# Attention with normed q and k, then an MLP: first groups scaled on VectorE, first group's norm in parts, transposes placed one score later

## The chip, the cores and the metric

The kernel runs on one core of one Trainium2 chip. A core has TensorE (PE; its weight loads are shown apart as PEld), VectorE (DVE), ScalarE (ACT), GpSimd (POOL), SyncE (SP), which issues transfers, and 16 DMA engines. The metric is the device time of one execution in microseconds; the time of a kernel is the median over several executions.

## The reference

```python
q_n, k_n = rmsnorm(q, g_q), rmsnorm(k, g_k)          # x / sqrt(mean(x*x) + 1e-6) * g
scores = 1.0 / sqrt(64) * q_n @ k_n^T                # 8 batches x 12 heads, 448 x 448
attn = exp(scores - max) / (sum(exp(scores - max)) + 1e-9)
x = (attn @ v) as [8 * 448, 12 * 64]                 # 3584 x 768
h = x @ w_in                                         # 3584 x 2048
g = max(h, 0) + alpha * min(h, 0)
out = g @ w_out                                      # 3584 x 768
```

All inputs and the output are fp32; the kernel computes its matmuls in fp16 and accumulates in fp32.

## The kernel before

A *group* y is four heads of one batch: three groups (G) make a batch, 24 the whole. Its q and its k are one tile `nat` each, 128 partitions by 896 elements, fp32. For each group the kernel squares q and k (`square`, L141), sums over the head dimension (`reduce`, L151, DVE), takes the inverse root on ACT as Ln and Exp (`root`, L159), multiplies into fp16 (`scale`, L168), and transposes. Groups 0 to 5 are transposed on PE (`turn`, L188, with copies out of PSUM that also multiply k by the gain g_q * g_k); later ones by DMA transposes that SP issues (`turn_dma`, L178), after which only the gain is left for DVE (L192).

Scores of a group come in seven key tiles j: `score` (L225) makes four matmuls into one of two PSUM tiles, `soft` (L243) one exp of 128 x 896 on ACT. The sums of the exps (`den`, L269), their inverse (`log`, `invert`) and attn @ v (`attv`, L285) follow for two groups together and then for the third of a batch. Then come the MLP's units: `up` (L344) makes one of 16 feature blocks ft of h (six matmuls), a multiple by alpha on ACT (L354) into one of three `ah` buffers, and a maximum on DVE (L355) into gT; `down` (L357) makes one output tile of 128 tokens x 384 columns (16 matmuls), a copy, and two output transfers. Two PSUM banks serve `up` and `down` in turn, a further pair (`hTa`, `opa`, `hTb`) now and then.

The order is written out by hand: the program is a list of *bursts* n of two to four scores, and dictionaries say what else belongs to a burst: `prep` ahead of it, `post` behind it, `jobs` between its units, `roots`, `turns`, `dens` and `avs` by burst, `gaps` its MLP units. Each engine runs its own instructions strictly in this order, and waits where an operand or a buffer is not ready. The *lead* burst, number 10, is where the first batch's attention ends and its first feature blocks, begun before, are finished.

Transfers stand in queues too. SP issues the loads of q and k (six `nat` buffers, so that a load waits until an earlier group's tile has been scaled), the DMA transposes and the output; each waits for one of eight completion slots, used in turn. Pool issues v and the weights between its own squares and scalings: w_in in four column blocks (`load_w_in`), w_out in four quarters (`load_w_out`: two row halves of the left 384 columns, then of the right), each quarter 768 KB in SBUF. Weights and v are cast to fp16 on the way, through the queue that the profile calls software_dynamic.

While little else runs, PE gets filler matmuls (`spin`, L390). Before the change the squares of groups 0 and 1 are on ACT, the others on Pool; of the scalings q of groups 1, 2 and 3 and k of group 0 are on DVE, the others on Pool.

Of the kernel before, what the change touches and what calls it, by code (L numbers as in the profile page):

```python
# [9 lines left out]
FP32 = mybir.dt.float32  # L10
# [11 lines left out]
def kernel(  # L22
# [118 lines left out]
    def square(y, nm):  # L141
        src = nat[y, nm].rearrange("p h j d -> p (h j d)")
        sq = ld.tile([128, 2 * J, D], FP32, name="sq", tag="sq", bufs=4)
        sqf = sq.rearrange("p n d -> p (n d)")
        if y < 2:
            nc.scalar.activation(out=sqf, in_=src, func=AF.Square)  # L146
        else:
            nc.gpsimd.tensor_mul(out=sqf, in0=src, in1=src)  # L148
        sqs[y, nm] = sq
# [17 lines left out]

    def scale(y, nm):  # L168
        t = ld.tile([128, J, 2, D], FP16, name="qs", tag="qs", bufs=4)
        eng = nc.vector if (y, nm) in ((0, "k"), (1, "q"), (2, "q"), (3, "q")) else nc.gpsimd  # L170
        eng.tensor_mul(  # L171
            out=t.rearrange("p j h d -> p h j d"),
            in0=nat[y, nm],
            in1=rr_t[y][:, "qk".index(nm)].unsqueeze(3).broadcast_to((128, 2, J, D)),
        )
        qs[y, nm] = t

    def turn_dma(y):  # L178
        for nm in "qk":
# [8 lines left out]
    def turn(y):  # L188

        if y >= TD:  # L190
            t = qkT[y, "k"].rearrange("p j g c -> p (j g c)")
            nc.vector.tensor_scalar(  # L192
                out=t, in0=t, scalar1=gain[:, 0:1], scalar2=None, op0=ALU.mult
            )
            return
        if y <= G:
            ps = [psf.tile([128, 512], FP32, name="tps", tag="mm") for _ in "qk"]
        else:
            ps2 = psa.tile([128, 2, 512], FP32, name="tps2", tag="acc")
            ps = [ps2[:, 0], ps2[:, 1]]  # L200
        tps = [
            t[:, : S].bitcast(FP16).rearrange("p (j c) -> p j c", j=J) for t in ps
        ]
        for tp, nm in zip(tps, "qk"):
            for j in range(J):
                nc.tensor.transpose(  # L206
                    tp[:, j, :], qs[y, nm][:, j].rearrange("p h d -> p (h d)"), ident
                )
        for tp, nm in zip(tps, "qk"):
            t = att.tile([128, J, 2, 64], FP16, name=f"{nm}T", tag=f"{nm}T", bufs=4)  # L210
            o = t.rearrange("p j g c -> p j (g c)")
            if nm == "q" and y == 0:
                nc.scalar.copy(out=o, in_=tp)
            elif nm == "q":
                nc.vector.tensor_copy(out=o, in_=tp)
            else:
                nc.vector.tensor_scalar(
                    out=o, in0=tp, scalar1=gain[:, 0:1], scalar2=None, op0=ALU.mult
                )
            qkT[y, nm] = t  # L220
# [114 lines left out]
    def begin(ft):  # L335
# [5 lines left out]
            begun[2], begun[3] = t[:, 0], t[:, 1]  # L341
        up_part(begun[ft], 0, ft, 0, G - 1)

    def up(b, ft, spare=False):  # L344
        if b == 0 and ft in begun:
            hT = begun[ft]

            for n in {2: (2, 3), 3: ()}.get(ft, (ft,)):
                up_part(begun[n], 0, n, G - 1, G)
        else:  # L350
            hT = bank("hT", spare)
            up_part(hT, b, ft, 0, G)
        ah = ffn.tile([128, S], FP16, name="ah", tag="ah", bufs=3)
        nc.scalar.activation(out=ah, in_=hT[:, :S], func=AF.Copy, scale=alpha_sb[:, ft : ft + 1])  # L354
        nc.vector.tensor_max(out=gT[:, ft, ds((b & 1) * S, S)], in0=hT[:, :S], in1=ah)  # L355

    def down(b0, t, oh, jobs=(), spare=False):  # L357

# [82 lines left out]
                last_in[y] = n  # L441
            m += 1
    NB = len(bursts)
    prep, post, roots = {}, {}, {}

    def at(n, f, *a):
        prep.setdefault(max(int(n), 0), []).append((f, a))
# [12 lines left out]
    for y in range(G, NG):  # L460

        early = y < G + 2
        if early:
            n = turn_at[y - 1] + 1
        elif y == G + 2:
            n = den_at[G - 1]
        elif y == 2 * G:
            n = turn_at[y] - 4
        elif y % G == 1:
            n = den_at[y - 4] - 1  # L470
        elif y % G:
            n = den_at[y - G]
        else:
            n = av_at[y - 4]
        at(n - (6 if early else 4 if y <= 3 * G else 5), load_qk, y)
        for nm in "qk":
            if y != 2 * G:
                after(n - 2, square, y, nm)
            if early:
                after(n, reduce, y, nm)  # L480
            else:
                jobs.setdefault(n, []).append((reduce, (y, nm)))
        roots[n + 1] = y
    for b in range(1, B):
        at(av_at[G * b] - 6, load_v, b)

# [86 lines left out]
    load_qk(1, True)  # L573
    load_qk(2)

    spin(3)
    spin(17, False)
    ct = psf.tile([128, 512], FP32, name="ct", tag="mm")
    nc.tensor.transpose(ct[:, : NF + 2], rows, ident32[: NF + 2, : NF + 2])
    spin(1)  # L580
    for nm in "qk":
        square(0, nm)
        reduce(0, nm)
    nc.vector.tensor_copy(out=cols, in_=ct[:, : NF + 2])
    for nm in "qk":
        root(0, nm)
        scale(0, nm)
    nc.vector.tensor_mul(
        out=gain, in0=cols[:, NF : NF + 1], in1=cols[:, NF + 1 : NF + 2]
    )  # L590
    square(1, "q")
    turn(0)
    square(1, "k")
    load_v(0)
    square(2, "q")
    for nm in "qk":
        reduce(1, nm)
    after(0, root, 1)
    for nm in "qk":
        after(0, scale, 1, nm)  # L600
    after(0, square, 2, "k")
    after(0, load_w_in, 0)
    for nm in "qk":
        after(2, reduce, 2, nm)
    after(5, load_w_in, 1)
    after(7, load_w_in, 2)
    after(8, load_w_in, 3)
# [1 line left out]
        after(first + (0, 0, 2, 4)[c], load_w_out, c)  # L609
    for nm in "qk":  # L610
        after(first, square, 2 * G, nm)
    roots[3] = 2

    since = 2
    for n in range(NB):
# [4 lines left out]
        lead = n == den_at[G - 1]  # L620
        first_tiles = tiles[: 2 if lead else split.get(n, 2)]
        for t in first_tiles:
            score(*t)
            if n == den_at[G - 1] - 1 and t == tiles[-1]:
                begin(0)
                begin(1)
            elif lead and t == tiles[0]:
                soft(*t)
                den(dens[n])
                attv(avs[n], 0, True, (log, invert))  # L630
            elif lead and t == tiles[1]:
                begin(2)
        plain = lead or n not in dens and n not in avs
        wait = plain and not lead and gaps[n] and gaps[n][0][0] is up
        if lead:
            begin(3)
        for t in tiles[:1] if wait else tiles[1:2] if lead else first_tiles:
            soft(*t)
        if n in dens and not lead:
            den(dens[n])  # L640
# [15 lines left out]
        if n in roots:  # L656
# [3 lines left out]

                late = [(2, score, tiles[2]), (2, soft, tiles[2])]
            if lead or wait and y < TD:
                late += [(4 if lead else 1, f, a) for f, a in work]
            else:
                for f, a in work:
                    f(*a)
# [30 lines left out]
        for k, (f, a) in enumerate(gaps[n]):  # L697
# [3 lines left out]
            else:  # L701
                f(*a, spare)
                done += 1
                if n in jobs and not (lead and done < 4):
                    g, c = jobs[n].pop(0)
                    g(*c)
                    if not jobs[n]:
                        del jobs[n]
                while late and done == late[0][0]:
                    _, g, c = late.pop(0)  # L710
                    g(*c)
        if not gaps[n] and n in turns:
            turn(turns[n])
        for _, g, c in late:
            g(*c)
# [36 lines left out]
```

## Time and profile before

| | us |
|---|---|
| median of 7 executions | 435.91 |
| lowest, highest | 432.19, 437.68 |
| the profiled execution | 437.68 |
| its span, first to last instruction | 435.8 |
| PE busy | 417.7 (96%) |
| ACT busy | 278.8 (64%) |
| DVE busy | 203.3 (47%) |
| POOL busy | 175.1 (40%) |
| first exp starts at | 13.66 |
| first `up` matmul starts at | 35.3 |

A row of the timeline has its start, its duration, engine, line, operation, output and inputs, count, and in brackets how long the engine was idle before it and what ended that. A row of a stretch of time has the busy time of PE, PEld, DVE, ACT and POOL, the granted share of TensorE's clock, the share of the 16 DMA engines, and GB/s. Shares of DMA over 1 mean that packets overlap in an engine. Profiled times are of one execution; its own 437.68 us is what they add up to, 1.9 us of it outside the span.

### The profile page before, as it was taken

What the parts mean: (1) busy time and instruction counts of PE and PEld (TensorE: products, weight loads), DVE (VectorE), ACT (ScalarE), POOL (GpSimd) and SP (SyncE); (2) the same over time, 40 slices, a digit from 0 to 9 for tenths busy, and PEclk for the clock granted to TensorE, in tenths of its full rate; (3) what the DMA queues carried; (4) which work ended last, traced back from release to release, by engine and by line L of the source; (5) the groups of instructions that cost most, each with busy time, mean ns of one, the idle gap of its engine ahead of it and who ended that gap; (6) DMA issues with size and microseconds to landing.
All of it is one profiled execution on the core that took longest, in us unless ns stands there. A gap on an engine that the chain in (4) does not pass through costs nothing.

```text
span 435.8 us, 11487 instructions
## 1 busy us (share of the span) xinstructions
PE 417.7 (96%) x4964; PEld 216.5 (50%) x4964; DVE 203.3 (47%) x304; ACT 278.8 (64%) x385; POOL 175.1 (40%) x133
## 2 busy tenths in 40 slices
PE   7789899789999999999999999999999999999996
PEld 3344344344455545554555545554555545555564
DVE  3755763444645363455445363555444354233421
ACT  4998888548877577757757587758757587122300
POOL 4799795366084605562093605562073000000000
PEclk9999999989999999999999999999999999999999
DMA  8999999999649752789139862775054300211133
GB/s 186 232 234 218 159 212 129 233 177 213 146 69 198 150 142 33 143 174 204 25 80 199 148 149 40 134 172 129 19 96 95 80 9 21 53 41 27 29 72 74
DMA packets 70387, 53.85 MB, mean 124 GB/s; under 512 B 37424, under 2 KB 70336, under 8 KB 70336
## 3 DMA queue, kind: packets, MB, share of 16 engines
q1 hardware_dynamic: 55536, 40.19, 43.8%
q0 software_dynamic: 13984, 11.81, 18.0%
q10 hardware_dynamic: 816, 1.11, 1.1%
q8 instruction: 39, 0.64, 0.7%
q14 instruction: 12, 0.10, 0.1%
HBM read 45.62 MB, written 11.01 MB: 130 GB/s over the span
## 4 chain that ended last, share of the span: by engine, by line
PE 83%; DMA 6%; ACT 5%; DVE 4%; issue 1%; POOL 0%; SPq 0%; ACTq 0%
PE op L365 27%; PE hT L327 21%; PE hTa L327 10%; PE sc L232 7%; PE opa L365 6%; DMA w_out_sb<-in_moe_w_out_dram 5%; PE av L261 5%; PE dn L261 4%; ACT expT L246 3%; PE avb L261 2%; DMA nat<-in_k_dram 1%; DVE ss L154 1%; PE tps L206 1%; DVE gT L355 1%; DVE osb L377 1%
## 5 line engine op out<-in xcount | busy, mean ns | idle before, releaser
L246 ACT ACTIVATE expT<-sc,expb 128x896 f16<-128x896 f32 x168 | 161.5, 1003 | 40.8 <-PE sc L232 39.9
L171 POOL TENSOR_TENSOR qs<-nat,rr 128x896 f16<-128x896 f32 x44 | 76.7, 1762 | 152.2 <-issue 94.8
L365 PE MATMUL op<-w_out_sb,gT 128*128 128x384 f16 (+1 forms) x752 | 126.5, 323 | 2.8 <-DMA w_out_sb<-in_moe_w_out_dram 2.8
L365 PEld LDWEIGHTS <-gT 128*128 128x128 f16 x912 | 85.8, 98 | 68.4 <-issue 15.9
L327 PEld LDWEIGHTS <-w_in_sb 128*128 128x128 f16 x768 | 73.1, 98 | 75.3 <-issue 11.0
L327 PE MATMUL hT<-xT,w_in_sb 128*128 128x448 f16 x510 | 107.1, 353 | 2.3 <-DVE gT L355 2.2
L354 ACT ACTIVATE ah<-hT,cols 128x448 f16<-128x448 f32 x85 | 53.7, 633 | 44.9 <-PE hT L327 44.9
L355 DVE TENSOR_TENSOR gT<-hT,ah 128x448 f16<-128x448 f32 x85 | 52.8, 623 | 52.2 <-ACT ah L354 52.2
L148 POOL TENSOR_TENSOR sq<-nat 128x896 f32<-128x896 f32 x44 | 72.9, 1678 | 9.6 <-DMA nat<-in_q_dram 6.9
L377 DVE COPY osb<-op 128x384 f32<-128x384 f32 (+1 forms) x47 | 25.8, 548 | 88.8 <-PE op L365 88.8
L232 PE MATMUL sc<-qT,kT 64*32 64x448 f16 (+1 forms) x1092 | 53.6, 357 | 5.0 <-ACT expT L246 2.8
L154 DVE TENSOR_REDUCE ss<-sq 128x14 f32<-128x896 f32 x48 | 50.5, 1077 | 9.5 <-ACT sq L146 6.1
L327 PE MATMUL hTa<-xT,w_in_sb 128*128 128x448 f16 x246 | 53.2, 352 | 0.0
L354 ACT ACTIVATE ah<-hTa,cols 128x448 f16<-128x448 f32 x41 | 26.0, 634 | 31.3 <-PE hTa L327 31.3
L355 DVE TENSOR_TENSOR gT<-hTa,ah 128x448 f16<-128x448 f32 x41 | 25.5, 623 | 26.0 <-ACT ah L354 26.0
L232 PEld LDWEIGHTS <-kT 64*32 64x32 f16 (+1 forms) x1092 | 15.2, 93 | 37.1 <-issue 30.6
L365 PE MATMUL opa<-w_out_sb,gT 128*128 128x384 f16 x160 | 27.7, 326 | 0.6 <-DVE xT L312 0.6
L261 PEld LDWEIGHTS <-vt 64*32 64x32 f16 (+1 forms) x1260 | 19.4, 95 | 14.1 <-issue 3.5
L312 DVE TENSOR_TENSOR xT<-av,rden 128x896 f16<-128x896 f32 x16 | 17.5, 1092 | 18.2 <-PE av L261 14.9
L261 PE MATMUL av<-expT,vt 64*32 64x448 f16 (+1 forms) x812 | 25.4, 357 | 0.0
L261 PE MATMUL dn<-expT,ones 64*32 64x448 f16 (+1 forms) x812 | 24.2, 350 | 0.9
L278 ACT ACTIVATE rden<-dn 128x896 f32<-128x896 f32 x16 | 14.5, 907 | 7.3 <-PE dn L261 7.3
(45 smaller groups left out, 158.8 us busy)
## 6 DMA issues: line engine op xcount, KB each, us to landing
out_dram<-osb SPq DMA_DIRECT2D x109, 96.0 KB, 2.3
nat<-in_q_dram SPq DMA_DIRECT2D x46, 224.0 KB, 5.3
nat<-in_k_dram SPq DMA_DIRECT2D x46, 224.0 KB, 6.6
vt<-in_v_dram POOLq DMA_DIRECT2D x16, 336.0 KB, 7.3
w_in_sb<-in_moe_w_in_dram POOLq DMA_DIRECT2D x12, 256.0 KB, 7.3
w_out_sb<-in_moe_w_out_dram POOLq DMA_DIRECT2D x4, 768.0 KB, 13.0
nat<-in_q_dram ACTq DMA_DIRECT2D x2, 224.0 KB, 5.0
nat<-in_k_dram ACTq DMA_DIRECT2D x2, 224.0 KB, 6.5
```

Source lines behind the costliest of these rows:

```text
L148: nc.gpsimd.tensor_mul(out=sqf, in0=src, in1=src)
L154: nc.vector.tensor_reduce(out=ss_t[y][:, "qk".index(nm)].rearrange("p h j -> p (h j)").unsqueeze(2), in_=sqs[y, nm], axis=AXIS_X, op=ALU.add,)
L171: eng.tensor_mul(out=t.rearrange("p j h d -> p h j d"), in0=nat[y, nm], in1=rr_t[y][:, "qk".index(nm)].unsqueeze(3).broadcast_to((128, 2, ...
L232: nc.tensor.matmul(out=sc[ds(64 * g + m * c, m), par, :S].rearrange("p (j c) -> p j c", j=J), lhsT=kT[ds(64 * par, 64), j, g, ts(c, m)], r ...
L246: nc.scalar.activation(out=expT[y][:, j], in_=scs[y, j][:, :, :S], func=AF.Exp, scale=QK_SCALE, bias=expb[:, 0:1],)
L261: nc.tensor.matmul(out=accs[g][ds(m * h, m), :S], lhsT=weights(g, y, par, ts(c, m), j), rhs=expT[y][ds(64 * g, 64), j, par, :], start=(j = ...
L312: nc.vector.tensor_mul(out=x, in0=av[:, :, :S], in1=r)
L327: nc.tensor.matmul(out=hT[:, :S], lhsT=w_in_sb[:, g * G + i, ts(ft, 128)], rhs=xT[b][:, g, i, :], start=(i == 0 and g == 0), stop=(i == G ...
L354: nc.scalar.activation(out=ah, in_=hT[:, :S], func=AF.Copy, scale=alpha_sb[:, ft : ft + 1])
L355: nc.vector.tensor_max(out=gT[:, ft, ds((b & 1) * S, S)], in0=hT[:, :S], in1=ah)
L365: nc.tensor.matmul(out=ops[c][:, :PW], lhsT=gT[:, ft, ts(t, 128)], rhs=w_out_sb[:, ft, ds(oh * OH + c * PW, PW)], start=(ft == 0), stop=(f ...
L377: nc.vector.tensor_copy(out=o[:, ts(c, PW)], in_=ops[c][:, :PW])
```

## The change

- The squares of group 0 and of q of group 1 stay on ACT; k of group 1 is squared by Pool.
- Both q and k of groups 1 and 2 are scaled by DVE, one after the other, and so is k of group 0; q of group 0 stays on Pool, and group 3 is as before. A copy of one element on Pool (`follow`) reads the end of k's scaled tile of groups 0, 1 and 2; Pool's later work stands behind it.
- Group 0 is worked on in parts: q's square and sum in two halves, k's whole chain for key tiles 0 to 2 first and 3 to 6 after. q's transposed copy goes from ACT to DVE. k's second part is transposed behind the first burst.
- The transposes of groups 1 and 2 are made right ahead of scores (1, 0) and (1, 6).
- In the MLP's first batch the alpha multiples of blocks 2 and 3 are made by DVE, and their maxima come behind block 4's. In the lead burst the root and scalings of group 4 come after two units in place of four; the second sum and the root of group 5 come one burst later.
- q and k of group 9 are loaded behind burst den_at[3] (17), after the transposes of group 7, where they were loaded ahead of burst 16, right behind group 8. The order in which SP issues becomes: transposes of 6, load of 8, two outputs, transposes of 7, two outputs, load of 9. v of batch 1 is issued by Pool ahead of the two scalings of group 5, where it was behind them.
- The first block of w_in is issued behind burst 1 for burst 0. One of the 20 filler matmuls at the start is of the narrow kind for the wide kind, one behind the gains' transpose is gone, one stands ahead of a transpose if a burst before den_at[0] has no units.

```diff
 def square(y, nm):
-        if y < 2:
+        if (y, nm) == (1, "q"):
             nc.scalar.activation(out=sqf, in_=src, func=AF.Square)
 def scale(y, nm):
-        eng = nc.vector if (y, nm) in ((0, "k"), (1, "q"), (2, "q"), (3, "q")) else nc.gpsimd
+        eng = nc.vector if y < G or (y, nm) == (G, "q") else nc.gpsimd
...
+    def part_square(nm, h, j, eng):      # on ACT, for heads h and key tiles j
+    def part_reduce(nm, h, j):
+    def part_root(nm, j):
+    def part_scale(nm, j, n, eng):
+    def part_turn(nm, js):
+    def part_copy(nm, j, eng):
...
+    mark = cst.tile([128, 1], FP16, name="mark", tag="mark")
+    def follow(y, nm):
+        nc.gpsimd.tensor_copy(out=mark, in_=qs[y, nm][:, J - 1, 1, D - 1 : D])
 def up(b, ft, spare=False):
+        if b == 0 and ft in (2, 3):
+            nc.vector.tensor_scalar(
+                out=ah, in0=hT[:, :S], scalar1=alpha_sb[:, ft : ft + 1], scalar2=None,
+                op0=ALU.mult,
+            )
+            held.append((hT, ah, ft))
+            return
         nc.scalar.activation(out=ah, in_=hT[:, :S], func=AF.Copy, scale=alpha_sb[:, ft : ft + 1])
-        nc.vector.tensor_max(out=gT[:, ft, ds((b & 1) * S, S)], in0=hT[:, :S], in1=ah)
+        for hT, ah, ft in [(hT, ah, ft)] + (held if b == 0 and ft == 4 else []):
+            nc.vector.tensor_max(out=gT[:, ft, ds((b & 1) * S, S)], in0=hT[:, :S], in1=ah)
...
-        at(n - (6 if early else 4 if y <= 3 * G else 5), load_qk, y)
+        if y == 3 * G:
+            after(den_at[G], load_qk, y)
+        else:
+            at(n - (6 if early else 4 if y <= 3 * G else 5), load_qk, y)
...
-                jobs.setdefault(n, []).append((reduce, (y, nm)))
-        roots[n + 1] = y
+                jobs.setdefault(n + (y == G + 2 and nm == "k"), []).append((reduce, (y, nm)))
+        roots[n + 1 + (y == G + 2)] = y
...
-    for nm in "qk":
-        square(0, nm)
-        reduce(0, nm)
+    K0 = 3
+    both, full, lo, hi = slice(0, 2), slice(0, J), slice(0, K0), slice(K0, J)
+    for h in range(2):
+        part_square("q", slice(h, h + 1), full, nc.scalar)
+    for h in range(2):
+        part_reduce("q", slice(h, h + 1), full)
+    part_root("q", full)
+    part_scale("q", full, J, nc.gpsimd)
+    part_square("k", both, lo, nc.scalar)
+    part_square("k", both, hi, nc.scalar)
+    part_reduce("k", both, lo)
+    part_reduce("k", both, hi)
+    part_root("k", lo)
+    part_scale("k", lo, K0, nc.vector)
+    part_root("k", hi)
+    square(1, "q")
...
+    part_turn("q", range(J))
+    part_turn("k", range(K0))
+    part_copy("q", full, nc.vector)
+    part_copy("k", lo, nc.vector)
+    load_v(0)
+    part_scale("k", hi, J - K0, nc.vector)
+    follow(0, "k")
+    square(1, "k")
+    reduce(1, "q")
+    square(2, "q")
+    after(0, part_turn, "k", range(K0, J))
+    after(0, part_copy, "k", hi, nc.vector)
+    after(0, reduce, 1, "k")
+    mid[1] = 1
+    after(1, square, 2, "k")
+    after(1, load_w_in, 0)
     for nm in "qk":
-        after(2, reduce, 2, nm)
+        after(3, reduce, 2, nm)
...
-    roots[3] = 2
+    mid[4] = 2
...
         for t in first_tiles:
+            if t in ((1, 0), (1, J - 1)):
+                turn(1 + (t[1] > 0))
             score(*t)
...
+            if n in mid and t == tiles[-1]:
+                root(mid[n])
+                for nm in "qk":
+                    scale(mid[n], nm)
+                follow(mid[n], "k")
             soft(*t)
...
-                late += [(4 if lead else 1, f, a) for f, a in work]
+                late += [(2 if lead else 1, f, a) for f, a in work]
...
-                if n in jobs and not (lead and done < 4):
+                if n in jobs and not (lead and done < 5):
```

## The prediction

> **What bounds the kernel now.** First I read the busy rows and the chain of the page: PE is busy 417.7 of 435.8 us and the chain is 83% PE, so what can be won is about 18 us of PE idleness, 4 of them after 300 us, in the tail. Next, the engines by stretch of time, to see where that idleness lies (us; PE busy, PEld, DVE, ACT, POOL; then granted clock, DMA share, GB/s):
>
> ```profile
> PE 83%; DMA 6%; ACT 5%; DVE 4%; issue 1%; POOL 0%; SPq 0%; ACTq 0%
> ...
> 12.00:30.00 18.00, 14.21 (x165) 6.07 (x163) 11.51 (x13) 16.95 (x23) 15.53 (x13) 1.00 1.17 234
> 42.00:50.00 8.00, 6.26 (x39) 2.53 (x37) 5.21 (x9) 6.62 (x12) 4.89 (x5) 1.00 0.96 144
> 50.00:66.00 16.00, 15.24 (x123) 7.53 (x122) 10.12 (x16) 13.43 (x22) 15.99 (x14) 1.00 1.19 207
> 66.00:88.60 22.60, 18.35 (x296) 9.36 (x293) 8.88 (x12) 15.58 (x19) 10.76 (x8) 1.00 1.28 182
> 88.60:96.00 7.40, 7.37 (x63) 3.75 (x63) 3.34 (x5) 3.34 (x5) 3.82 (x5) 0.77 1.06 147
> ```
>
> From 12 to 30 us ACT is full (16.95 of 18); from 50 to 66 Pool is (15.99 of 16); from 66 to 88.6 the DMA engines are (share 1.28) and PE is idle for 4.25 us. From 96 to 300 us PE is idle for 0.6 us in all. So whatever reaches PE has to pass 88.6 us, where the chain has 21 us of transfer. The timeline there, and at two earlier places (start, duration, engine, instruction, idle before it):
>
> ```profile
> 48.80 1.30 PE L327 MATMUL hT<-xT,w_in_sb 128*128 128x448 f16 x6 [1.74 <-DVE gT L355]
> ...
> 78.30 0.38 PE L232 MATMUL sc<-qT,kT 64*64 64x448 f16 x4 [0.71 <-DVE kT L192]
> 79.30 2.76 PE L365 MATMUL opa<-w_out_sb,gT 128*128 128x384 f16 x16 [0.62 <-DVE xT L312]
> ...
> 88.63 1.50 PE L365 MATMUL op<-w_out_sb,gT 128*128 128x384 f16 x8 [2.80 <-DMA w_out_sb<-in_moe_w_out_dram]
> ...
> 90.81 2.74 PE L261 MATMUL av<-expT,vt 64*64 64x448 f16 x28
> ```
>
> PE is ready at 85.83 and waits 2.80 us for the last quarter of w_out (issued by Pool at 67.61). Then its clock drops: av takes 2.74 us where the same 28 took 1.49 at 38.78, and the eight scores beside it 0.96 for 0.57: 1.6 us more. Without stall and drop this execution is 437.68 - 2.80 - 1.6 = 433.3; the seven runs lie in two heaps, 432.19 to 433.51 and 435.91 to 437.68, as if some miss the stall. Last, the queues in 2 us windows (MB, share of 16 engines; q0 carries w_out and v, q1 q, k, output and transposes), at 68, 72 and 82 us:
>
> ```profile
> q0 software_dynamic: 368, 0.28, 89.5%
> q1 hardware_dynamic: 386, 0.10, 36.8%
> ...
> q1 hardware_dynamic: 456, 0.12, 129.5%
> q0 software_dynamic: 24, 0.02, 5.6%
> ...
> q1 hardware_dynamic: 217, 0.35, 69.9%
> q0 software_dynamic: 195, 0.15, 47.8%
> ```
>
> Alone q0 moves 0.41 MB in such a window (58 to 66 us). Beside the first packets of group 6's transposes (T6) it keeps 0.28; then, 70 to 76 us, T6 holds the engines and w_out gets 0.02; from 77 to 86 it shares with q and k of groups 8 and 9, at 0.15. That is why the last quarter (0.79 MB) takes 21 us.
>
> **What the Trainium skill says.** GPSIMD Engine Reference, Key points: Pool shares its SBUF interfaces with VectorE and contends with DVE instructions that have two SBUF inputs. The trace agrees: Pool's scaling takes 1.69 us alone (at 9.19) and 2.59 beside a DVE scaling (at 16.10), while its squares beside reductions stay at 1.68. ScalarE: Activation LUTs, What ACT_TABLE_LOAD costs: an ACTIVATE is a fixed part and 0.833 ns an element; the traced square of 896, 0.95 us, makes 448 elements 0.57 by that slope (estimate). TensorE: Matmul & The Clock Gate, What's actually happening: an idle window of about 3.4 us, free-running, halves the clock; the trace has the drop after 2.80 us and none after 1.74. DMA: Bandwidth & Descriptors, Issuing engines are not separate DMA queues: all interleave on 16 engines, as the windows show.
>
> **The change, part by part.** Durations are those of this trace; a shorter operand is scaled by its elements over a fixed 0.15 to 0.2 us.
>
> *First group in parts.* q lands at 5.42. Two half squares end at 6.0 and 6.5, their reductions (half of 1.09) at 6.65 and 7.2, root at 7.8, Pool's scaling at 9.5, against 10.88: the root no longer stands behind k's square. k lands at 7.71: squares of 3 and 4 tiles to 8.9, reductions to 9.6, scaling of 3 tiles (0.55) to 10.2, ten transposes to 10.5; cols, gain and both copies (0.17, 0.15, 0.62, 0.33) to 11.5. First score 11.55 for 13.22: 1.65 us. ACT sheds a square (0.95, to Pool) and a copy (0.91, to DVE).
>
> *Where that goes.* k's rest is scaled by 12.2; only then does the new one-element copy on Pool (named follow) let Pool square k of group 1 (1.68, to 14.05); behind it on Pool wait that square, q of group 2 and later the first w_in issue. Reduction to 15.1, root to 15.65. ACT has done three exps (0.94 each) by 14.9 and stalls 0.2. DVE now scales q and k in turn, 2 x 1.09, to 17.9 (before: both at once on two engines, to 18.7); transposes behind score (0,6) to 19.05; copies to 19.85. Exp (1,0) starts at 20.3 for 20.63: 0.3 us left. Group 2 likewise: root at 22.55, scaled by 25.3, transposes to 26.5, score, filler matmul (0.95), and exp (2,0) at 28.2 against 28.1. So by 30 us I take the lead as nil. Bounds: 0.3 us worse, if copies and squares slow each other; 1.65 better, if all of it holds.
>
> *Lead burst (42 to 52 us).* The root of group 4 comes two units earlier: ACT has it behind the exp that ends at 44.7, done at 45.3 for 47.03. Pool's queue waits on it (3.11 us idle), so its scalings, the first two w_out issues, all that follows and the q loads of SP that wait for it come 1.75 us sooner; from 47 to 68 Pool never idles, so this lasts. v of batch 1 is issued before two scalings; q0 is full then, and it costs nothing. The two copies on DVE (0.62 each) cost ACT 1.27 less, and ft 4's maximum runs ahead of the held two: done at 46.6 for 48.75, so PE's 1.74 us wait goes. Next late is ft 7, behind the scores: 1.1 us lead. Root 5, now later on ACT, takes some back where ACT is nearly full (13.43 of 16): I take 1.0 at 66 us, bounds 0.4 and 1.7.
>
> *DMA stage.* T6 lands at 76.0 for 77.8, so the 0.71 wait goes and the 0.62 stays (xT waits for it): PE reaches the last quarter at 85.83 - 1.6 = 84.2. The quarter is issued at 65.9, and T6 is through at about 74.5. Then q and k of group 8 (0.92 MB) and w_out share as at 82 us: group 8 is done at 80, w_out has 0.43 MB and lacks 0.33. Group 9's load, moved behind the transposes of group 7 (T7), is out of the way. But T7, in the trace issued at 83.10 behind group 9's loads, which wait for free completion slots, now issues at 73 to 76 and follows group 8 in the ring. If T7 starts as T6 did (q0 kept 0.28 MB in 2 us), 0.33 MB take 2.3 us: 82.3, before PE is there. If T7 holds the engines as T6 did at 70 to 76, w_out waits. I take the first; both ends are kept.
>
> *Sum.* No stall (2.80), no drop (1.6), arrival 1.6 earlier: 437.68 - 6.0 = 431.7 us. Against the median of 435.91, which holds the stall, 4.2 us or 1.0% less.
>
> **Rivals.** *T7 takes group 9's place.* For: 70 to 76 us, where T6 left q0 0.02 MB. T7 from 80 to 86.5, then 0.33 MB at the shared 0.16 in 2 us less what trickled: about 88. PE stands 3.8 us and the clock drops: 437.68 - 0.6 = 437.1, or some 436.4 with the trickle; no change. Against: T7 alone took 3.2 us later in the run (124 to 127). *The front's gain holds.* For: ACT is the bound there. Against: the scaling chain above. 431.7 - 1.65 = 430.0. *Slower: T7 smothers w_out.* T6's packets beside w_out spanned 66 to 77.8, 11.8 us. From 80 that is 91.8, plus 0.33 MB at 0.2 MB a us: 93.4, 4.8 us later than now: 442.5. It decides from a landing at 91.3. For: same ring, same place. Against: T6 met two quarters, T7 half of one. *The roots are not earlier* (ACT late at 44.7): Pool keeps its times, which ends in one of the first two cases.
>
> **How the numbers follow.** Forecast 0.50 (430.8 to 433.5), T7 in group 9's place 0.28 (435.3 to 437.8), front holds 0.12 (430.0), smothered 0.10. A measurement of this kernel tells about 1% from no change: faster means below 431.55, slower above 440.3. Slightly under half of the forecast's case lies below 431.55 (0.23), with the front 0.35; smothered 0.10; the rest 0.55. The range, 430.0 to 437.5, leaves out the last case and the edge of the second.
>
> **What would show it.** Right: first exp near 12.0 but exp (2,0) still near 28; no wait at ft 6; w_out's first issue near 48.6; the second half of op at 84 to 85 without a DMA wait and with full clock behind it. Wrong: a DMA wait over 2 us at that op with T7's small packets beside it; or q0 and T7 sharing the engines evenly, but exp (2,0) later than 29, which would mean that DVE's two scalings in turn cost more than Pool's hold frees.

## The result, and the profile after

| | before | after |
|---|---|---|
| median, us (executions) | 433.22 (64) | 434.50 (27) |
| lowest, highest | 431.14, 439.04 | 431.02, 437.33 |
| ratio of after to before | | 1.0021, 95% interval 1.0006 to 1.0036 |
| the profiled execution, its span | 437.68, 435.8 | 434.08, 432.1 |

The change makes no difference of 1%; the interval leaves a small loss, 0.1 to 0.4%. The 64 executions of the kernel before include the seven shown ahead of the prediction, whose median of 435.91 was high. So was their profiled execution, a slow one, 1.5% above the fastest of the 64: a second profile of the unchanged kernel (below, "the kernel before once more") has a span of 431.0 us. Medians of the kernel before differ by a few tenths of a microsecond from one group of runs to the next, so I compare by ratios. A ratio is not the quotient of the two medians: here the two differ by as much as 0.0025 (the lead edits below have a ratio of 0.9999, by medians 1.0015), so differences smaller than that say little.

The same views of the changed kernel: first the shares of the chain that ended last.

```profile
PE 80%; DMA 6%; DVE 4%; ACT 4%; POOL 3%; issue 1%; SPq 1%; ACTq 1%; POOLq 0%
```

Then its engines by stretch of time (us; busy PE, PEld, DVE, ACT, POOL; granted clock, DMA share, GB/s).

```profile
12.00:30.00 18.00, 13.61 (x178) 6.02 (x185) 13.12 (x15) 15.95 (x23) 12.41 (x14) 1.00 1.14 244
42.00:50.00 8.00, 7.83 (x64) 3.80 (x63) 7.08 (x12) 6.87 (x11) 7.06 (x8) 1.00 1.07 177
50.00:66.00 16.00, 15.18 (x109) 7.36 (x108) 10.96 (x17) 14.10 (x22) 15.97 (x12) 1.00 1.23 202
66.00:88.60 22.60, 20.54 (x334) 10.31 (x332) 8.61 (x13) 15.88 (x19) 6.69 (x4) 1.00 1.29 183
88.60:96.00 7.40, 5.89 (x39) 2.85 (x38) 3.32 (x5) 3.35 (x8) 5.92 (x5) 1.00 1.03 221
```

The lead burst is fuller (42 to 50 us: PE busy 7.83 for 6.26). In the transfer stage, 66 to 88.6 us, PE is busy for 20.54 us, more than the 18.35 of the first profile of before, which holds the stall, but less than the 22.28 of the second, which has none. And from 88.6 to 96 us PE now stands for 1.5 us, and in neither profile of before does it stand there. PE's timeline of the changed kernel at these places (start, duration, instruction, and in brackets the idle time before it with what ended it):

```profile
49.03 1.30 PE L393 MATMUL hT<-xT,w_in_sb 128*128 128x448 f16 x6
...
76.11 0.38 PE L298 MATMUL sc<-qT,kT 64*64 64x448 f16 x4
77.11 2.76 PE L442 MATMUL opa<-w_out_sb,gT 128*128 128x384 f16 x16 [0.62 <-DVE xT L378]
...
84.46 1.46 PE L442 MATMUL op<-w_out_sb,gT 128*128 128x384 f16 x8 [0.82 <-DMA w_out_sb<-in_moe_w_out_dram]
...
95.03 2.62 PE L393 MATMUL hT<-xT,w_in_sb 128*128 128x448 f16 x12 [1.51 <-DVE osb L454]
...
98.31 1.29 PE L393 MATMUL hT<-xT,w_in_sb 128*128 128x448 f16 x6 [0.16 <-DVE gT L432]
```

The 1.74 us wait of the lead burst is gone, the one on the last quarter of w_out is 0.82 for 2.80 with full clock behind it, and at 95.03 there is a new wait of 1.51 us, for the copy `osb`. VectorE's and then Pool's timeline of the changed kernel show what held that copy:

```profile
91.79 1.09 DVE L154 TENSOR_REDUCE ss<-sq 128x14 f32<-128x896 f32 x1 [2.83 <-POOL sq L148]
93.43 1.09 DVE L154 TENSOR_REDUCE ss<-sq 128x14 f32<-128x896 f32 x1 [0.55 <-POOL sq L148]
94.43 0.55 DVE L454 COPY osb<-op 128x384 f32<-128x384 f32 x1
```

```profile
90.08 3.32 POOL L148 TENSOR_TENSOR sq<-nat 128x896 f32<-128x896 f32 x2 [6.72 <-DMA nat<-in_q_dram]
```

Group 9's q arrives only at 90 us. Its squares wait for it on Pool, its sums wait for the squares on VectorE, and the copy that frees a bank for PE stands behind the sums.

Last, the queues of the changed kernel in 2 us windows at 66, 68, 72 and 82 us (packets, MB, share of the 16 engines):

```profile
q0 software_dynamic: 369, 0.28, 89.3%
q1 hardware_dynamic: 403, 0.10, 37.5%
...
q1 hardware_dynamic: 655, 0.16, 85.3%
q0 software_dynamic: 206, 0.15, 48.1%
...
q1 hardware_dynamic: 141, 0.05, 61.8%
q0 software_dynamic: 137, 0.11, 57.7%
...
q1 hardware_dynamic: 390, 0.10, 85.6%
q0 software_dynamic: 65, 0.05, 17.7%
```

Group 6's transposes (T6) no longer push w_out to nothing at 72 us, but neither queue moves much there: 0.16 MB in 2 us for the two together, against 0.38 at 66 us.

### The profile page after: what moved, and what is told of

It is laid out like the page before. It is cut to its first block, busy times and chain, and to the rows that moved or that the text cites. A ratio compares the mean times of both kernels' runs of the same rounds, so it can differ in the third digit from the quotient of the medians.

```text
span 432.1 us, 11497 instructions
## 1 busy us (share of the span) xinstructions
PE 415.7 (96%) x4961; PEld 216.1 (50%) x4961; DVE 206.9 (48%) x313; ACT 276.7 (64%) x385; POOL 172.0 (40%) x135
## 4 chain that ended last, share of the span: by engine, by line
PE 80%; DMA 6%; DVE 4%; ACT 4%; POOL 3%; issue 1%; SPq 1%; ACTq 1%; POOLq 0%
PE op L442 26%; PE hT L393 20%; PE hTa L393 10%; PE sc L298 6%; PE opa L442 6%; PE dn L327 4%; PE av L327 4%; DMA kT<-qs 3%; PE avb L327 2%; POOL sq L148 2%; DMA nat<-in_q_dram 2%; DVE ss L154 1%; ACT expT L312 1%; DMA nat<-in_k_dram 1%; DVE osb L454 1%
## 5 line engine op out<-in xcount | busy, mean ns | idle before, releaser
L171 POOL TENSOR_TENSOR qs<-nat,rr 128x896 f16<-128x896 f32 x41 | 69.7, 1721 | 138.4 <-issue 92.0
L148 POOL TENSOR_TENSOR sq<-nat 128x896 f32<-128x896 f32 x45 | 74.5, 1676 | 12.8 <-DMA nat<-in_q_dram 6.7
L154 DVE TENSOR_REDUCE ss<-sq 128x14 f32<-128x896 f32 x46 | 48.6, 1077 | 6.2 <-POOL sq L148 6.0
L327 PE MATMUL av<-expT,vt 64*32 64x448 f16 (+1 forms) x812 | 24.5, 350 | 0.5 <-issue 0.5
```

Source lines behind the costliest of these rows:

```text
L154: nc.vector.tensor_reduce(out=ss_t[y][:, "qk".index(nm)].rearrange("p h j -> p (h j)").unsqueeze(2), in_=sqs[y, nm], axis=AXIS_X, op=ALU.add,)
L171: eng.tensor_mul(out=t.rearrange("p j h d -> p h j d"), in0=nat[y, nm], in1=rr_t[y][:, "qk".index(nm)].unsqueeze(3).broadcast_to((128, 2, ...
L327: nc.tensor.matmul(out=accs[g][ds(m * h, m), :S], lhsT=weights(g, y, par, ts(c, m), j), rhs=expT[y][ds(64 * g, 64), j, par, :], start=(j = ...
```

## The experiments

Three reasons stand against each other: the moved load of group 9 costs what the rest wins; what is won ahead of 64 us is taken back by transfers that land no sooner; or the changed front lets TensorE's clock fall, which some profiles show and that of the changed kernel doesn't. I call the *front* everything up to 40 us (norm in parts, VectorE's scalings, Pool held, transposes one score later, fillers), and the *lead edits* the two multiples on VectorE, the earlier root of group 4 and the later sum and root of group 5, with what moves along: Pool's scalings, w_out's quarters and v of batch 1 are issued sooner.

### Group 9's load

*Put back behind group 8's, the rest as changed.*

```diff
-        if y == 3 * G:
-            after(den_at[G], load_qk, y)
-        else:
-            at(n - (6 if early else 4 if y <= 3 * G else 5), load_qk, y)
+        at(n - (6 if early else 4 if y <= 3 * G else 5), load_qk, y)
```

> The changed kernel with one part undone: group 9's q and k are loaded where they were before, right behind group 8 and ahead of the transposes of group 7. Theory A (the gain of about 2.2 us up to the last w_out quarter is spent 10 us later, where DVE waits for the sums of group 9 and holds back the copy that frees PE's bank): the 1.51 us wait of PE on that copy shrinks below 0.5 us, but the quarter shares the engines with group 9 again and lands near 86, so PE waits 2 to 2.5 us there; 434 to 436 us, ratio to before 1.000 to 1.006. Theory B (the transposes of group 7, now ahead, hold the quarter back): the wait for the quarter is below 0.5 us, and the time 431.5 to 432.5.

Measured: 434.03 us, ratio to before 1.0017 (0.9997 to 1.0037). The wait at 95 us is gone, but the one on the quarter is back at 2.44 us and k of group 6 is waited for (0.84):

```profile
76.50 0.38 PE L298 MATMUL sc<-qT,kT 64*64 64x448 f16 x4 [0.84 <-DVE kT L260]
...
86.47 2.00 PE L442 MATMUL op<-w_out_sb,gT 128*128 128x384 f16 x8 [2.44 <-DMA w_out_sb<-in_moe_w_out_dram]
```

So the move trades one wait for another.

*Moved alone, in the kernel before* (the same lines the other way round).

> The kernel before with one part of the change alone: q and k of group 9 are loaded behind the transposes of group 7. Theory A (DVE's wait for group 9's sums costs): 0.5 to 1.5 us more than before, 433.8 to 434.7, with PE waiting for the copy or a maximum near 96 us. Theory D: the transposes of group 7 come 6 us sooner and group 9 2 us later, neither is waited for long, since PE is 2 us later here than in the changed kernel: 433.0 to 433.7.

Measured: 435.06 us, 1.0031 (1.0011 to 1.0050). Its profile has the wait of the changed kernel and no other above 0.2 us from 66 to 100 us; the load costs 1.3 us by the ratio (0.5 to 2.2):

```profile
94.49 2.62 PE L327 MATMUL hT<-xT,w_in_sb 128*128 128x448 f16 x12 [1.04 <-DVE osb L377]
```

*The copy ahead of group 9's two sums on VectorE, in the changed kernel.*

```diff
         for f, a in jobs:
-            if f is not turn:
+            if f is not turn and a[0] != 3 * G:
                 f(*a)
         o = ffn.tile([128, OH], FP32, name="osb", tag="osb", bufs=4)
...
         for f, a in jobs:
-            if f is turn:
+            if f is turn or a[0] == 3 * G:
                 f(*a)
```

> The changed kernel with DVE's order altered in one place: the two sums of group 9 stand behind the copy out of PSUM of the same unit, not ahead of it. Theory A: the 1.51 us wait of PE on that copy is gone, 0.3 to 0.6 us of it may come back two units later where a maximum stands behind the sums; 433.0 to 433.6 us where the changed kernel has 434.5, ratio to before 0.998 to 1.000. Theory B (the wait for w_out is what spends the gain): no more than 0.3 us, ratio 1.002.

Measured: 435.19 us, 1.0020 (0.9996 to 1.0044). The wait is not gone but moved on to 97.95 us, to a maximum that now stands behind the same sums:

```profile
97.95 1.29 PE L393 MATMUL hT<-xT,w_in_sb 128*128 128x448 f16 x6 [1.62 <-DVE gT L432]
```

No time came back, against the expectation of 433.0 to 433.6 us. So the copy's place isn't the cause; with the load put back the wait is gone, with the load moved alone it comes, so the late arrival is.

### The kernel before once more

No edit.

> The kernel before once more, unchanged, for its profile and for what a comparison of equal kernels gives. Theory A: most of its executions have no long wait for the last w_out quarter; the profile shows a wait below 1.5 us there, full clock behind it and an own time of 432 to 434 us; ratio 1.000 within 0.002. Rival: the wait of 2.8 us is in most executions, and the median of 433.2 holds it; then the profile shows it again beside a time of about 433.

Measured: 433.53 us, 1.0003 (0.9981 to 1.0024). Its profile shows what the first one hid. These are all of PE's waits that it names from 60 to 100 us:

```profile
61.14 1.29 PE L327 MATMUL hT<-xT,w_in_sb 128*128 128x448 f16 x6 [0.42 <-DVE gT L355]
...
66.66 0.38 PE L232 MATMUL sc<-qT,kT 64*64 64x448 f16 x4 [0.17 <-ACT expT L246]
...
97.25 1.29 PE L327 MATMUL hT<-xT,w_in_sb 128*128 128x448 f16 x6 [0.15 <-DVE gT L355]
```

No wait on w_out, none on kT, and no drop of the clock: the stall of 2.80 us belonged to that one execution. Beside it the changed kernel (both at full clock in this stage) reads so, by the starts of the same instructions on PE:

| | before once more | after | difference |
|---|---|---|---|
| ft 7 of the lead burst | 52.17 | 49.03 | -3.14 |
| first output tile | 66.98 | 63.90 | -3.08 |
| opa, behind k of group 6 | 78.68 | 77.11 | -1.57 |
| first h matmul behind w_out's last quarter | 91.67 | 91.08 | -0.59 |
| h behind `osb` | 93.97 | 95.03 | +1.06 |
| span | 431.0 | 432.1 | +1.1 |

The change does win 3 us in this execution, and loses them in three places: 1.5 us at the transposes of group 6, 1.0 at the last quarter, 1.65 at group 9. Of the 1.5, 0.84 stand in the profile as a pause inside av (72.07 to 74.35 us) for which it names no cause, and 0.69 ahead of opa; but k's gain runs to 76.06 and the score that needs it starts at 76.11, so without the pause PE would have waited there. Behind 96 us nothing more happens. Where the clock falls in the front, less is won: with the copy ahead of the sums, the same program up to here, the score ahead of the first output tile starts at 65.49 us, for 63.58 in this profile and 66.66 in the second of before.

### Transfers

*Quarters 3 and 4 of w_out issued one and two bursts after the first two, in the changed kernel.*

```diff
-        after(first + (0, 0, 2, 4)[c], load_w_out, c)
+        after(first + (0, 0, 1, 2)[c], load_w_out, c)
```

> The changed kernel with the third and fourth quarter of w_out issued one and two bursts behind the first pair, for two and four. The fourth is in place by about 81 us. Theory A: no wait for w_out, the wait of PE on the copy near 95 stays at 1.5 us or more; 432.9 to 434.0 us. Theory B: the time falls to 431.5 to 432.5, since what the executions lose is the wait for w_out.

Measured: 433.87 us, 1.0009 (0.9990 to 1.0028). The waits on the quarter and on `osb` are gone; k of group 6 is late instead (PE waits 1.56 us at 78.12), and the clock is at half in opa behind it (4.44 us for 2.76). The time fits theory A, but the wait that it names at 95 us isn't there: the loss has moved again.

*The lead edits alone, in the kernel before; and the front alone* (the changed kernel with lead edits and group 9's load undone).

> The kernel before with the edits of the lead burst alone (two multiples on DVE, root of group 4 two units sooner, sum and root of group 5 one burst later). Full clock as before. By the prediction's steps 1.0 to 1.7 us won: 431.5 to 432.3. Theory D: the first w_out issue is 1.7 us sooner and PE is 1.5 us ahead at 60 us, but k of group 6 lands within 0.5 us of where it does before, and PE then waits for it or for the last quarter: 432.7 to 433.4.

> The kernel before with the front of the change alone (first group in parts, q and k of groups 1 and 2 on DVE, transposes one score later, fewer fillers), the lead burst and group 9's load as before. Theory C: mean clock under 0.997 in more than half of the executions, time 433.4 to 434.5, no better than before. Theory D: first MLP unit up to 1.5 us sooner, nothing of it left at 96 us, 433.0 to 433.6. By the prediction's own steps: 0 to 0.3 us won, 432.9 to 433.3, full clock.

Measured: lead edits 433.62 us, 0.9999 (0.9976 to 1.0022); front 434.39 us, 1.0022 (1.0000 to 1.0043). The first gains nothing that can be told from noise, although every step of it works: SP issues k's transpose of group 6 at 62.42 us for 65.29 in the kernel before once more. These are that issue and, on VectorE, the gain that follows the landing, first in the lead edits alone and then in the kernel before once more:

```profile
62.42 3.98 SPq L181 DMA_TRANSPOSE kT<-qs  x1
...
77.30 0.45 DVE L192 TENSOR_SCALAR kT<-kT,gain 128x896 f16<-128x896 f16 x1 [4.53 <-DMA kT<-qs]
```

```profile
65.29 3.32 SPq L181 DMA_TRANSPOSE kT<-qs  x1
...
75.72 1.54 DVE L192 TENSOR_SCALAR kT<-kT,gain 128x896 f16<-128x896 f16 x1 [0.40 <-DMA kT<-qs]
```

Issued 2.9 us sooner, landed 1.6 us later, and PE waits 1.92 us for it. One execution of each would not be enough, but the other profiles agree. From this issue to the gain it takes 13.27 to 14.88 us in all six kernels that have the lead edits, T6 on the DMA and every load. Without the lead edits it takes 9.95 to 11.07 us in six profiles; the seventh, the first of before, has 13.36. What lengthens it is open: w_out's third quarter is issued 4.3 us ahead of it and the fourth 3.2 us behind it in both kernels, while v of batch 1 comes at 53.42 us for 59.63, ahead of a scaling.

*The same two kernels with less to transfer.* No q and k of group 9, no v of batch 1.

```diff
     def load_qk(y, hold=False):
+        if y == 3 * G:
+            for nm in "qk":
+                nat[y, nm] = nat[y - 1, nm]
+            return
...
     def load_v(b):
+        if b == 1:
+            vt[1] = vt[0]
+            return
```

> The lead burst's edits alone on the kernel before, with two transfers left out: q and k of group 9 and v of batch 1 are not loaded, group 8's and batch 0's tiles are used for them, so that the result is another one there; 1.6 of the 18.6 MB up to 95 us are saved, all else is as it was. Theory D (the lead of 1.5 to 3 us at 60 us is lost to arrivals of transfers between 64 and 92 us): PE's waits for k of group 6 (1.92 us) and the last quarter (0.49) fall below 0.3 us, the lead reaches 96 us, and the time is 430.0 to 431.7 us. If the lead is lost to something else on the engines: 432.5 to 433.6, as with all transfers.

> The kernel before with the same two transfers left out (group 9 uses group 8's q and k, batch 1 uses batch 0's v). Theory D: in most executions the kernel before doesn't wait for these transfers, so little comes of it, 432.2 to 433.2 us, and it is 1 to 2 us slower than the lead burst's edits with the same transfers. If the kernel before is bound by transfers itself: under 432.

Measured: lead edits 430.27 us, 0.9909 (0.9878 to 0.9941); kernel before 431.88 us, 0.9952 (0.9932 to 0.9972). With the same loads gone from both, the lead edits are worth 1.6 us by medians and 1.9 by ratios, about what the prediction had for the earlier arrival at the last quarter. Neither profile has a wait on PE between 67 us and 90 us, and opa, first with the lead edits and then without, keeps the lead:

```profile
76.41 2.77 PE L383 MATMUL opa<-w_out_sb,gT 128*128 128x384 f16 x16
```

```profile
78.30 2.77 PE L372 MATMUL opa<-w_out_sb,gT 128*128 128x384 f16 x16
```

So the lead is lost to transfers. Which of the two left out takes it isn't separated.

*Group 6 transposed on TensorE*, which takes T6 out of the stage and leaves the computation whole; with the lead edits, in the kernel before, and with the whole change but for group 9's load.

```diff
-    TD = min(6, NG)
+    TD = min(7, NG)
...
-        turned = n in turns and gaps[n] and (turns[n] >= TD or turns[n] < 2 * G)
+        turned = n in turns and gaps[n] and (turns[n] >= TD or turns[n] < TD)
```

> The lead burst's edits alone, and group 6 transposed by PE as groups 0 to 5 are, not by DMA transposes: 14 transposes more on PE (0.95 us) and two copies on DVE (1.3 us), no DMA transposes before group 7's. Theory D: no wait for k of group 6, the last quarter in place 4 us or more sooner, 1.5 us of lead reach 96 us less 0.95 of PE: 431.5 to 432.8 us. If transfers are not what takes the lead: 434.0 to 434.8, the price of the transposes added.

> The kernel before with group 6 transposed on TensorE alone. Theory (the DMA transposes of group 6 hold the stage from 66 to 80 us, and the lead burst's edits are worth 1.6 us once they are out of the way): 432.6 to 433.2, so that the lead burst's edits make the rest of the way to 431.07. Rival (the gain of the earlier run was group 6's move alone): 430.8 to 431.5.

> The changed kernel with group 9's load back behind group 8's, and group 6 transposed on TensorE in place of the DMA. Theory: the front gains nothing that lasts beyond 30 to 40 us in most executions (0.7 us at the third exp of group 2 in the changed kernel's profile) and lets the clock drop to half in most of them, 1.3 us each. Then this is no faster than the lead edits with group 6 on TensorE (431.07): 431.0 to 432.3, with a mean clock below 0.997 in more than half of the executions. Rival: the front's lead was only lost to the transfers like the rest; then it comes on top, 429.5 to 430.5.

Measured: with the lead edits 431.07 us, 0.9941 (0.9916 to 0.9967); in the kernel before 432.06, 0.9969 (0.9954 to 0.9984); with the front too 431.78, 0.9964 (0.9941 to 0.9987). The first is the fastest kernel here that computes all, ahead of both kernels of this case. Its queues in the windows at 66 and 72 us:

```profile
q1 hardware_dynamic: 192, 0.31, 68.3%
q0 software_dynamic: 190, 0.16, 50.7%
...
q0 software_dynamic: 412, 0.32, 101.3%
q1 hardware_dynamic: 115, 0.14, 26.2%
```

Without T6 the two queues move 0.46 to 0.47 MB in 2 us, where the changed kernel has 0.16 at 72 us, and 0.52 at 76 us when T6 is through. Two things change here at once: T6 leaves the DMA engines, and SP, which issued it, comes to the loads behind it sooner (groups 8 and 9 at 56.93 and 61.17 us, for 66.45 and 69.59 with the lead edits alone). What each is worth isn't separated. The split between the edits falls between the two expectations: group 6's move is worth 1.1 us to the kernel before by medians against the same runs, and the lead edits add about 1.0, with intervals that overlap. The front adds nothing: where the mean clock is at least 0.997 (7 of 22 executions) the kernel with the front has a median of 430.94, the one without 431.06; in the other 15 it has 432.21.

### The clock

In the profiles of six kernels with the changed front TensorE's clock falls to half for some us between 11 and 30 us; the changed kernel's own profile and that of the front alone have none of it. This is the stretch from 20 to 23 us in the run with the copy ahead of the sums, and then in the changed kernel, the same program up to here:

```profile
20.00:23.00 3.00, 2.93 (x14) 0.82 (x14) 2.00 (x3) 1.01 (x1) 1.76 (x3) 0.50 1.11 248
```

```profile
20.00:23.00 3.00, 2.55 (x16) 0.70 (x16) 1.73 (x3) 2.71 (x5) 1.60 (x3) 1.00 1.11 264
```

The mean clock of each execution tells how often it falls, though not where: in the first profile of before, with a mean of 0.995, it falls behind the stall at 88.6 us.

| kernels | executions with mean clock below 0.997 |
|---|---|
| before, beside all experiments | 35 of 277 |
| group 9's load alone, lead edits alone | 4 of 22, 7 of 22 |
| group 6 on TensorE: before, with lead edits | 0 of 22, 0 of 14 |
| group 6 on TensorE, lead edits and front | 15 of 22 |
| front alone | 16 of 22 |
| the changed kernel | 23 of 28 |

With and without the front, group 6 on TensorE and the lead edits in both, the count is 15 of 22 against 0 of 14: the front does it. In the front alone those executions have a median of 434.58 us, the others 433.28: 1.3 us. In the changed kernel it is 434.52 against 433.89, so at full clock too it is no faster than the kernel before. Three edits looked for the part of it that does this.

*Two narrow fillers more between the scores of each early burst, in the changed kernel.*

```diff
             score(*t)
+            if n < den_at[0] and t == tiles[0]:
+                spin(2, False)
```

> The changed kernel with two narrow filler matmuls between the two scores of each of bursts 0 to 6, where PE waits for exps. Theory C (the changed front leaves PE so idle between 8 and 25 us that its clock drops to half in most executions, which costs 1 to 1.9 us by 35 us): the mean granted clock returns to 0.998 or more in most executions, and 1.0 to 1.5 us come back, 433.0 to 433.6 us. Theory D (what is won before 64 us is lost again to arrivals of transfers, k of group 6, the last w_out quarter, group 9): the clock returns, but under 0.5 us of time, 434.0 to 434.6.

*The front alone with the fillers ahead of the first transposes as they were.*

```diff
-    spin(2)
-    spin(18, False)
+    spin(3)
+    spin(17, False)
...
+    spin(1)
     K0 = 3
```

> The changed front alone, with the filler matmuls ahead of the first transposes as they were in the kernel before (three wide, 17 narrow, one wide behind the gains' transpose). Theory C (with that filler gone the clock drops by chance in the first 25 us): mean clock 0.998 or more in most executions, where the front alone had it in 6 of 22, and 432.7 to 433.4 us for 434.4. If the idle stretches between the scores make the drop, and not the filler: clock still under 0.997 in more than half, 434.0 to 434.8.

*The front alone with the scalings of groups 1 and 2 as they were.*

```diff
-        eng = nc.vector if y < G or (y, nm) == (G, "q") else nc.gpsimd
+        eng = nc.vector if (y, nm) in ((0, "k"), (1, "q"), (2, "q"), (3, "q")) else nc.gpsimd
...
-                follow(mid[n], "k")
```

> The front alone (as in the earlier run of it, 434.39, mean clock below 0.997 in 16 of 22 executions), with k of group 1 and k of group 2 scaled by Pool again beside VectorE's scaling of q, and without the one-element copies of Pool behind groups 1 and 2. Theory that the clock drops because VectorE's two scalings in turn keep TensorE waiting between scores of groups 1 and 2: clock below 0.997 in fewer than a third, time 433.0 to 433.7. Rival, that it is the order of the first group's parts and the transposes one score later: clock as in the front alone, more than half below 0.997, time 434 to 434.8.

None brings the clock back. Fillers between scores: 435.67 us, 1.0060 (1.0038 to 1.0082), below 0.997 in 15 of 22, and the fillers themselves cost time, since the other seven have a median of 435.42; its profile has full clock to 37 us and 0.57 from 37 to 41, behind 4 us in which PE was busy for 2.28. Fillers as before: 435.20, 1.0027 (0.9998 to 1.0057), 10 of 14. Scalings as before: 435.12 (434.52 without two executions above 439), 1.0035 (1.0013 to 1.0058), 16 of 22. In the last two the clock fits the rival (idle stretches between the scores in the one, the order of the front's work in the other), which doesn't show that the rival is the cause. The last run asked the reverse: does less work on PE alone bring the drop?

*The kernel before without the wide filler that follows the early bursts.*

```diff
-        if n < den_at[G - 1] - 1 and plain and n not in turns:
-            spin(1)
```

> The kernel before without the wide filler matmul (1.02 us in two passes) that follows each early burst without units, so that TensorE is idle for some 6 us more between 14 and 28 us and nothing else is changed. Theory that the clock drops in the changed front because TensorE is too little busy there (1.86 of 3 us busy at 17 to 20 us and 1.96 at 23 to 26 in the changed kernel, against 2.40 and 1.87 before): mean clock below 0.997 in more than half of the executions, median 433.8 to 435. Rival (idleness of this kind does not matter, the drop has another cause): clock below 0.997 in at most a quarter of the executions as in the kernel before, median 432.8 to 433.4.

Measured: 435.89 us, 1.0075 (1.0049 to 1.0101), more than either side expected, and below 0.997 in 22 of 22. Stretches of its profile and then of the kernel before once more, with their columns as above:

```profile
14.00:17.00 3.00, 0.82 (x12) 0.22 (x8) 2.10 (x3) 2.97 (x5) 2.08 (x2) 1.00 1.26 214
17.00:20.00 3.00, 2.46 (x21) 1.62 (x21) 0.79 (x2) 2.87 (x4) 3.00 (x2) 0.50 1.16 239
```

```profile
14.00:17.00 3.00, 2.48 (x16) 0.86 (x12) 2.09 (x3) 2.97 (x5) 2.08 (x2) 1.00 1.23 217
17.00:20.00 3.00, 2.40 (x27) 1.22 (x26) 1.36 (x3) 2.93 (x5) 3.00 (x2) 1.00 1.18 238
```

From 14 to 17 us PE is busy for 0.82 us, with ACT, VectorE and Pool as before, and half clock follows up to 33 us. Only the fillers were taken out, so too little work on PE is enough to set it off. That it is the cause in the changed front too fits its stretches (14 to 17 us: 1.65 of 3 busy; 17 to 20: 1.86; before once more 2.48 and 2.40), but is argued only: no edit of the front brought the clock back, and the run with the copy ahead of the sums had the drop behind 1.81 us of work from 14 to 17, more than the 1.65 of the changed kernel's profile, which had none.

## Why the prediction was wrong

The forecast was 431.7 us, 1.0% less than before; it is 434.5, 0.2% more. Three steps failed. The stall and the drop of the clock, 4.4 of the 6.0 us in the sum, were counted as a gain of the change, though a usual execution has neither. The earlier issue of T6 was counted as an earlier landing. And group 9's moved load was costed at nothing. In the profile the lead of 3.1 us over a usual execution is 0.6 at the last quarter, where 1.6 was forecast, and behind group 9 it is a loss of 1.1.

- *Base: failed for the ratio, held in us.* "Without stall and drop this execution is 437.68 - 2.80 - 1.6 = 433.3" is right, and it is what the kernel before usually takes (433.2). But the 4.4 us then stood in the sum as a gain of the change. They were a property of one profiled execution. The two heaps of the seven times were seen, "as if some miss the stall", and it wasn't concluded that the larger set of executions does. That leaves 1.6 us, "arrival 1.6 earlier", to be won from a usual execution.
- *First group and front: held in kind.* First score at 11.22 us (11.55 forecast), exp (2,0) at 27.41 for 28.13, so a lead of 0.7 where nil was taken, within its bounds. What was left out is the clock: its mean is lowered in 23 of 28 executions, and in the front alone the executions that have this are 1.3 us slower.
- *Lead burst: held, and was larger.* Root of group 4 on ACT at 43.84 to 44.43 us (45.3 forecast), w_out's first issue at 47.79 for 50.39, no wait at ft 6, ft 7 2.3 us sooner than in the first profile of before and 3.1 sooner than in the second (1.1 forecast).
- *"T6 lands 76.0 for 77.8": the number came out, its reason failed.* k's gain starts at 75.61. But the 77.8 is of a profile in which T6 was slow, 13.4 us from k's issue to its gain. The kernel before had 75.72 in its second profile, 10.4 us behind an issue 3.4 us later than that of the changed kernel (65.29 for 61.87). An earlier issue was taken to be an earlier landing; with the lead edits T6 takes 3 us longer, and 1.5 us of the lead was lost on this step. That the forecast number was met is luck.
- *Quarter: between the two ends.* T7 was issued at 72.31 and 76.46 us (73 to 76 forecast) and PE was at the quarter at 83.63 (84.2). "If T7 starts as T6 did (q0 kept 0.28 MB in 2 us)" was the wrong choice: q0 kept 0.05 at 82 us, and the quarter let PE go on at 84.46, where its landing was expected at 82.3. For PE the two errors nearly cancel, 84.46 for 84.2. (Of 0.79 MB, 0.43 being through, 0.36 are lacking and not 0.33: 0.2 us.)
- *"Group 9's load ... is out of the way": failed.* Costed at nothing, it costs 1.3 us alone. Its landing at 90 us is followed by Pool's squares, VectorE's sums and the copy in one chain, and PE waits for the last of them. Who waits for a moved transfer, through which in-order queues, was not followed to the end.
- *Rivals.* T7 did hold w_out back, but PE waits 0.82 us there, with full clock, not the 3.8 us of T7 in group 9's place or the longer wait of w_out smothered, and the front's lead doesn't hold. (The "about 88" of the first rival is too early for the rate that it names: 0.33 MB at 0.16 in 2 us behind 86.5 end at 90.6, less the trickle.) The case that happened, group 9 itself late, wasn't among them.

The three parts alone multiply to 1.0022 x 0.9999 x 1.0031 = 1.0052, more than the 1.0021 of the whole; each is known to about 0.002. Their waits are in the same stage, and group 9's move frees the quarter that the front alone waits for (2.10 us at 85.69), so they need not add.

## What to carry to other kernels

Before a stall in one profiled execution is put into a sum as the gain of a change, ask whether the other executions have it: where the times lie in two heaps, the profile belongs to one of them, and the change is to be judged against the usual one. A lead won ahead of a stage that waits on transfers is worth only what lands sooner, so look for the transfer that occupies the stage and remove or replace it (here six tenths of a per cent, with group 6's transposes on TensorE and the lead edits), rather than issue everything earlier. And a moved load is to be followed through every in-order queue behind its first reader, down to the engine that sets the end.

## What the runs showed of the hardware

- A DMA transpose issued 2.9 us sooner (62.42 for 65.29 us) landed 1.6 us later (77.30 for 75.72), with weight transfers in the other queue; from its issue to the gain behind it 13.27 to 14.88 us passed in the six profiles with the lead edits, and 9.95 to 11.07 in six of the seven without. While it ran in the changed kernel, both queues together moved 0.16 MB in 2 us (at 72 us); with these transposes on TensorE they moved 0.46.
- Half clock came without a long idle stretch. The Trainium skill, TensorE: Matmul & The Clock Gate, What's actually happening, has the clock fall after an idle window of about 3.4 us. Here 0.82 us busy in 3 us, in stretches of idleness under 1 us each, were followed by half clock in the profile, in a kernel that shows a low mean clock in all 22 executions; in the front's profiles about half of the time busy was followed by it in some executions and not in others. Which share decides is open: 1.59 of 3 us, from 11 to 14 us in the kernel before once more, and 1.87, from 23 to 26, were not followed by it. Nor does the length of one wait decide: behind 2.10 us in the front alone op ran at full clock (1.46 us), behind 1.56 and 0.61 us with the quarters sooner opa ran at half (4.44 for 2.76).
- One unchanged kernel showed a 2.80 us wait for a transfer in one execution and none in another, with 437.68 and 432.89 us.
